# Attention, a gated feed-forward layer and a second one in one kernel: operands moved to multiples of 128 bytes, masks put ahead of the scores

## The chip, the cores and the metric

The kernel runs on one core of a Trainium2 chip. The metric is the device time of one execution in microseconds: 475.54 us, the median of three runs (475.52 to 476.49).

## The reference

Three stages follow each other. The sizes are batch 2, 12 heads, 448 positions, 64 numbers a head; 896 tokens of 768; hidden sizes 1536 and 1024.

```python
scores = (1 / sqrt(64)) * q @ k.T          # per batch and head, 448 x 448
scores = where(upper triangle, -1e9, scores)
attn = exp(scores - max(scores)); attn = attn / (sum(attn) + 1e-9)
x = (attn @ v) as 896 tokens x 768

gate = sigmoid(x @ w_gate); val = x @ w_val
x = (gate * val) @ w_out                   # 768 -> 1536 -> 768

h = x @ w_in2                              # 768 -> 1024
solu = h * softmax(h)
ln = (solu - mean(solu)) / sqrt(var(solu) + 1e-6) * g_ln
out = ln @ w_out2                          # 1024 -> 768
```

All weights come as 64-bit floats. The kernel loads them as pairs of 32-bit words and makes 32-bit floats of them by bit operations.

## The kernel before, in words

**Products.** Most matrix products are made of three terms: each operand is split into a part in the rounded 32-bit format fp32r (called hi) and the rest (lo), and hi x hi, hi x lo and lo x hi are added in PSUM. x (tiles xy), the weight chunks (hl), the gated values (g), w_in2 (wi), w_out2 (wo) and the transposed normed values (lt) are kept as such pairs.

**Attention** (lines 204 to 566) works on twelve pairs of heads, p = 0 to 11. The positions are cut into four query tiles i = 0 to 3, which need the first 64, 192, 320 and 448 keys (causal mask). For each pair:

- `sc_mask` (L320) writes the mask of some tiles into PSUM, as small bf16 products; `sc_dots` (L336) adds the scores. Tiles 3 and 0 share one PSUM tile of two banks, tiles 2 and 1 another; the pool `ps_s` has two such PSUM tiles, so a pair's masks write what the pair before has just been read from. Both heads of a pair run side by side in the two halves of TensorE's rows. From pair 3 on, tiles 1 to 3 use the three terms (tiles qks), tile 0 plain fp32 in two passes.
- `sc_max` (VectorE, L351) takes the maxima, `sc_exp` (ScalarE, L363) the exponentials into p_t with their sums, in the order of tiles 3, 0, 2, 1.
- `sums` (GpSimd), `recips` (VectorE, L371 and L372) and DMAs over DRAM (`rs_rows`, `rs_bcast`) make the reciprocals of the sums and spread them.
- `tr_mm` (TensorE, L408) transposes p_t in four units u = 0 to 3; `tr_copy` copies each unit out of PSUM, units 0 and 1 on VectorE (L419), 2 and 3 on ScalarE (L417). The units use three PSUM buffers in turn.
- `pv_mm` (TensorE, L431) multiplies with v, `x_mul` (VectorE, L437) by the reciprocals, `x_hi` (ScalarE, L441) and `x_lo` (GpSimd, L447; VectorE for the last pair) split the result into xy.
- `prep_q`, `prep_hi` and `prep_lo` (GpSimd) scale and split q and k of the pair to come.

**Order.** The table `STEPS` (L481) writes the order out by hand: an entry is a step, an engine, a function and a range of pairs, and the function runs for pair p at step 8 p + its first number. Each engine works through its own queue in that order; waits between engines are put in where data or buffers ask for them. Into this order the making of the first four weight chunks is woven: `FIRST_BITS` (steps at which one of the four bit operations of a chunk is issued: L118 on ScalarE, then L121, L123 and L126 on VectorE), `FIRST_HI` (L139, ScalarE) and `FIRST_LO` (L144, VectorE), and `EARLY` (steps at which some products of the next stage, L463, go to TensorE). The first three pairs are issued by hand ahead of the table (L499 to L528).

**Filling products.** `keep_warm` (L290) issues products of zeros: 31 at the start, 6 behind the scores of pair 0, and 8 ahead of the first transposes (L405).

**Later stages.** L601 multiplies x with w_gate and w_val, chunk by chunk; L631 the gated values with w_out; `h_mm` (L663) with w_in2; `ln_T` (L706) transposes, and `out_mm` (L724) multiplies with w_out2, in blocks of 48 products for each of seven token tiles.

**Where tiles lie.** Tiles of a pool lie one behind the other in each partition, in multiples of 32 bytes. Pools on the left begin with `const`, whose seven tiles take 512 + 512 + 256 + 512 + 256 + 32 + 32 = 2,112 bytes, 64 more than a multiple of 128. So xy, the weight rings (hl) and g, and later wo, e and the first token tile's lt, start 64 past a multiple of 128. The pools on the right (qkr, qks, `one`; later w_in2 and the other lt in `w2`) end 32 bytes below a multiple of 128, so qkr, qks and wi start 96 past one. In the pool `one`, q_sc and v_raw start at multiples of 128, p_t 32 past one.

The two lines that the change of order is about, and the ones that set an order by hand:

```python
(0, 'E', lambda p: sc_mm(p, (0, 1)), 3), (2, 'E', lambda p: sc_mm(p, (1,)), 2, 3),
(23, 'A', x_hi), (15, 'A', lambda p: tr_copy(p, 2, 'A'), 1),
(12, 'D', lambda p: tr_copy(p, 0, 'D'), 2), (21, 'D', x_mul), (14, 'D', lambda p: tr_copy(p, 1, 'D'), 1),
```

Of the kernel before, what the change touches and what calls it, by code (L numbers as in the profile page):

```python
# [10 lines left out]
F32 = mybir.dt.float32  # L11
# [8 lines left out]
B, H, S, D = 2, 12, 448, 64  # L20
# [3 lines left out]
NQ = 4  # L24
QE = [64, 192, 320, 448]
POFF = [0, 128, 512, 1152, 2048]
# [17 lines left out]
def attn_moe_moe2(ctx: ExitStack, tc: tile.TileContext, qk, v, w_gv, w_out, w_in2, w_out2, g_ln, out):  # L44
# [19 lines left out]
    mhalf = const.tile([128, 1], F32, name="mhalf")  # L64

# [138 lines left out]
    with ExitStack() as actx:  # L204
# [12 lines left out]
        SPLIT = range(3, NH // 2)  # L217
# [29 lines left out]
        q_sc = [one.tile([128, D + S], F32, name=f"qs{i}") for i in range(2)]  # L247
        v_raw = [one.tile([128, NQ, 2 * D], F32, name=f"vr{i}") for i in range(3)]
# [30 lines left out]
        p_t = [one.tile([128, POFF[NQ]], F32, name=f"p{i}") for i in range(2)]  # L279

        mx0 = {(i, e): one.tile([128, 1], F32, name=f"mx{i}{e}") for i in (0, 1, 3) for e in range(2)}

        def groups(p):
            return GROUPS if p else ((1, 0), (3,), (2,))
# [39 lines left out]
        def sc_dots(p, g):  # L324
            k = qk_raw[p][:, 1]
            for i in groups(p)[g]:
                n = QE[i]
                if p not in SPLIT or i == 0:
                    terms = [(q_sc[p % 2][:, n - D:n + D], k)]
                else:  # L330
                    t = qk_sp[p]
                    terms = [(t[:, a, n - 128:n], t[:, b]) for a, b in ((0, 2), (0, 3), (1, 2))]
                for m, (l, r) in enumerate(terms):
                    for e in range(2):
                        rows = slice(e * D, (e + 1) * D)
                        nc.tensor.matmul(out=ps_sc[p, i][1 - e], lhsT=l[rows], rhs=r[rows, S - n:] if e else r[rows, :n],  # L336
                                         start=False, stop=(m == len(terms) - 1), skip_group_check=True)

        def sc_mm(p, gs):
            for g in gs:  # L340
                sc_mask(p, g)
                sc_dots(p, g)
# [60 lines left out]
        def tr_mm(p, u):  # L403
            ps = ps_tr[p, u] = ps_t.tile([128, 512], F32, tag="t", name="t")
            if p == u == 0:  # L405
                keep_warm(ps, 8)
            for c, k in tr_blocks(u):
                nc.tensor.transpose(ps[:, max(c, 0):max(c, 0) + 128], p_t[p % 2][:, k:k + 128],  # L408
                                    ident if c >= 0 else identx)
# [42 lines left out]
        def early_tiles():  # L452

            for t in range(NE):
                g_t[t] = gpa.tile([128, 2, NT], FR, tag=f"g{t}", name=f"g{t}")
                for i in range(2):
                    ps = ps_s.tile([128, 2, 512], F32, tag="s", name="gv")[:, 0, :S]
                    for kk in range(NK):
# [15 lines left out]
        FIRST_BITS = {40: (0,), 44: (0, 0), 52: (0,), 72: (1,), 76: (1, 1), 84: (1,),  # L474
                      96: (2,), 97: (2,), 99: (2,), 101: (2,), 104: (3,), 105: (3,), 107: (3,), 109: (3,)}
        FIRST_HI, FIRST_LO = {56: 0, 88: 1}, {60: 0, 92: 1}
# [5 lines left out]
            (0, 'E', lambda p: sc_mm(p, (0, 1)), 3), (2, 'E', lambda p: sc_mm(p, (1,)), 2, 3),  # L482
# [4 lines left out]
            (16, 'A', lambda p: tr_copy(p, 3, 'A'), 1), (16, 'D', lambda p: tr_copy(p, 3, 'D'), 0, 1),  # L487
            (1, 'A', lambda p: sc_exp(p, (3,)), 2), (2, 'A', lambda p: sc_exp(p, (0,)), 2),
            (5, 'A', lambda p: sc_exp(p, (2,)), 1), (6, 'A', lambda p: sc_exp(p, (1,)), 1),
            (23, 'A', x_hi), (15, 'A', lambda p: tr_copy(p, 2, 'A'), 1), (14, 'D', lambda p: tr_copy(p, 2, 'D'), 0, 1),  # L490
            (8, 'D', recips), (9, 'D', lambda p: tr_copy(p, 0, 'D'), 1, 2), (-1, 'D', lambda p: sc_max(p, 3, 0), 2, 3), (0, 'D', lambda p: sc_max(p, 3, 0), 3),
            (2, 'D', lambda p: sc_max(p, 2), 2), (3, 'D', lambda p: sc_max(p, 1), 2),
            (12, 'D', lambda p: tr_copy(p, 0, 'D'), 2), (21, 'D', x_mul), (14, 'D', lambda p: tr_copy(p, 1, 'D'), 1),
            (7, 'P', sums, 1), (-8, 'P', prep_q, 3), (23, 'D', x_lo, NPR - 1), (-8, 'P', prep_hi, SPLIT.start, SPLIT.stop), (-7, 'P', prep_lo, SPLIT.start, SPLIT.stop),
# [6 lines left out]
        for g in range(3):  # L501
            sc_dots(0, g)
# [36 lines left out]
        for s in range(PER * NPR + 26):  # L539
# [18 lines left out]
            if s in (76, 84):  # L558
                dma_next()
# [235 lines left out]
```

## Time and profile before

| | us |
|---|---|
| median of three runs | 475.54 |
| the profiled execution | 476.21 |
| its span, first to last instruction | 474.3 |
| attention, until the products of L601 begin | 91.1 |
| TensorE busy | 468.5 |
| VectorE busy | 309.2 |
| ScalarE busy | 206.2 |
| GpSimd busy | 103.2 |

The profile is of one execution. PE is TensorE's products, PEld its weight loads, DVE VectorE, ACT ScalarE, POOL GpSimd, SP the engine that issues DMAs. The length of a product's row runs from its start to its modelled end, and products overlap in the pipe, so the spacing of starts is what they cost each other. TensorE has the granted clock 1.0 in all of the 40 slices of the page. The 1.9 us between the span and the time of the execution lie outside the first and last instruction.

### The profile page before, as it was taken

Reading aid. Unit: us, or ns where it says so; the run is one execution under the profiler, and the core shown is the slowest. Engines: PE = TensorE matmul, PEld = TensorE weight load, DVE = VectorE, ACT = ScalarE, POOL = GpSimd, SP = SyncE. Lnnn points to the kernel's source line nnn. Section 1 sums busy time; section 2 is a strip of 40 time slices with the busy share of each in tenths; the row PEclk is TensorE's granted clock in tenths of the full one; section 3 lists DMA queues with packets and bytes.
Section 4 is the critical chain, followed back from the end, with each engine's and each line's share of the span. In section 5 each row is a group of like instructions: output and inputs, shape, how many; then the busy total and the mean of one; then the engine's idle time right before and its main releaser. Section 6 shows DMA issues by size and latency. Waiting matters only on the chain.

```text
span 474.3 us, 7187 instructions
## 1 busy us (share of the span) xinstructions
PE 468.5 (99%) x2761; PEld 413.7 (87%) x2761; DVE 309.2 (65%) x476; ACT 206.2 (43%) x439; POOL 103.2 (22%) x156
## 2 busy tenths in 40 slices
PE   8999999999999999999999999999999999999997
PEld 6677766899999999999999999999988888999997
DVE  5879898457567797777875667667618888712110
ACT  5798987433335435344353243433223334332111
POOL 2588992100000000000000000000423768500000
PEclk9999999999999999999999999999999999999999
DMA  7465654322314445335453233453412230001001
GB/s 225 132 198 184 186 170 136 102 79 101 133 56 166 165 145 170 99 131 178 133 178 133 80 129 102 157 177 134 158 43 66 80 120 1 2 35 66 35 33 66
DMA packets 16546, 55.56 MB, mean 117 GB/s; under 512 B 2816, under 2 KB 5888, under 8 KB 16512
## 3 DMA queue, kind: packets, MB, share of 16 engines
q1 hardware_dynamic: 16512, 55.11, 34.9%
q8 instruction: 21, 0.34, 0.3%
q14 instruction: 13, 0.11, 0.1%
HBM read 52.30 MB, written 2.80 MB: 116 GB/s over the span
## 4 chain that ended last, share of the span: by engine, by line
PE 91%; POOL 3%; DMA 2%; DVE 1%; issue 1%; ACT 1%; SPq 0%; DVEq 0%; POOLq 0%; ACTq 0%
PE gv L601 35%; PE pm L631 18%; PE po L724 12%; PE h L663 12%; PE x L431 4%; PE t L408 3%; PE s L336 2%; DMA qkr<-in_qk_dram 2%; PE gv L463 2%; PE tp L706 1%; POOL qks L239 1%; POOL qks L234 1%; POOL qs L242 0%; POOL xy L447 0%; PE s L320 0%
## 5 line engine op out<-in xcount | busy, mean ns | idle before, releaser
L601 PE MATMUL gv<-xy,hl 128*128 128x448 f32 x828 | 168.1, 366 | 0.0
L601 PEld LDWEIGHTS gv<-xy,hl 128*128 128x128 f32 x828 | 155.6, 188 | 12.5 <-issue 0.4
L631 PE MATMUL pm<-g,hl 128*128 128x448 f32 x432 | 87.7, 366 | 0.0
L631 PEld LDWEIGHTS pm<-g,hl 128*128 128x128 f32 x432 | 81.2, 188 | 6.3
L648 POOL TENSOR_SCALAR t<-t,g_sb 128x768 f32<-128x768 f32 x8 | 9.0, 1123 | 253.6 <-PE pm L631 253.6
L144 DVE TENSOR_TENSOR hl<-t,hl 128x768 fp32r<-128x768 f32 x36 | 34.9, 969 | 39.8 <-ACT hl L139 38.1
L724 PE MATMUL po<-wo,lt 128*128 128x384 f32 x336 | 60.6, 340 | 0.0
L663 PE MATMUL h<-wi,xy 128*128 128x512 f32 x252 | 59.3, 396 | 0.0
L724 PEld LDWEIGHTS po<-wo,lt 128*128 128x128 f32 x336 | 58.7, 188 | 0.2 <-POOL wo L653 0.2
L663 PEld LDWEIGHTS h<-wi,xy 128*128 128x128 f32 x252 | 47.2, 188 | 11.3
L123 DVE SCALAR_TENSOR_TENSOR t<-raw,t 128x768 int32<-128x768 int32 (+1 forms) x56 | 54.3, 970 | 1.9
L126 DVE SCALAR_TENSOR_TENSOR t<-raw,t 128x768 int32<-128x768 int32 (+1 forms) x56 | 53.0, 946 | 1.6
L118 ACT ACTIVATE raw<-raw 128x768 f32<-128x768 f32 (+1 forms) x56 | 48.3, 870 | 11.1 <-DMA raw<-in_wo_dram 6.8
L363 ACT ACTIVATE p<-s,sum 128x320 f32<-128x320 f32 (+3 forms) x90 | 41.4, 487 | 7.3 <-DVE sum L351 5.6
L121 DVE TENSOR_SCALAR t<-raw 128x768 int32<-128x768 int32 (+1 forms) x56 | 31.7, 565 | 6.1 <-ACT raw L118 6.0
L181 DVE TENSOR_TENSOR lt<-tp,lt 128x512 fp32r<-128x512 f32 x14 | 9.7, 690 | 36.4 <-ACT lt L180 36.4
L139 ACT CAST hl<-t 128x768 fp32r<-128x768 f32 x36 | 30.0, 833 | 4.2 <-PE pm L631 4.2
L193 ACT ACTIVATE wk<-gv 128x448 f32<-128x448 f32 x23 | 11.3, 541 | 43.4 <-PE gv L601 43.4
L431 PE MATMUL x<-pt,vr 128*64 128x384 f32 (+3 forms) x168 | 28.6, 410 | 0.0
L351 DVE TENSOR_REDUCE sum<-s 128x2 f32<-128x640 f32 (+3 forms) x43 | 26.7, 678 | 0.6 <-ACT pt L417 0.3
L139 ACT CAST wi<-t 128x512 fp32r<-128x512 f32 x12 | 7.5, 621 | 42.3 <-DVE t L126 42.3
L408 PE MATMUL t<-ident,p 128*128 128x128 f32 x180 | 24.5, 277 | 0.3 <-DVE pt L419 0.3
(95 smaller groups left out, 438.1 us busy)
## 6 DMA issues: line engine op xcount, KB each, us to landing
raw<-in_gv_dram SPq DMA_DIRECT2D x22, 768.0 KB
raw<-in_wo_dram SPq DMA_DIRECT2D x20, 768.0 KB
raw<-in_wi_dram SPq DMA_DIRECT2D x12, 512.0 KB
qkr<-in_qk_dram SPq DMA_DIRECT2D x11, 448.0 KB
vr<-in_v_dram SPq DMA_DIRECT2D x12, 256.0 KB
rb<-rd SPq DMA_DIRECT2D x24, 112.0 KB
out_dram<-o SPq DMA_DIRECT2D x6, 384.0 KB
raw<-in_gv_dram SPq DMA_DIRECT2D x8, 192.0 KB
```

The costliest lines, as they stand in the source:

```text
L118: nc.scalar.activation(out=w1.bitcast(F32), in_=w1.bitcast(F32), func=AF.Copy, scale=2.0 ** -112)
L123: nc.vector.scalar_tensor_tensor(out=tt, in0=w1, scalar=-2 ** 31, in1=tt, op0=ALU.bitwise_and, op1=ALU.bitwise_or)
L126: nc.vector.scalar_tensor_tensor(out=tt, in0=w0, scalar=29, in1=tt, op0=ALU.logical_shift_right, op1=ALU.bitwise_or)
L139: nc.scalar.copy(out=hi, in_=t_t[it])
L144: eng.tensor_tensor(out=lo, in0=t_t.pop(it), in1=f32(hi), op=ALU.subtract)
L363: nc.scalar.activation(out=p_t[p % 2][:, POFF[i] + (1 - e) * n:POFF[i] + (2 - e) * n], in_=ps_sc[p, i][1 - e], func=AF.Exp, bias=mx, scale ...
L408: nc.tensor.transpose(ps[:, max(c, 0):max(c, 0) + 128], p_t[p % 2][:, k:k + 128], ident if c >= 0 else identx)
L431: nc.tensor.matmul(out=ps_pv[pr][d, q0:], lhsT=v_raw[pr % 3][:, (j - 1) % NQ, d], rhs=pt_t[pr][:, u, c0:c0 + S - q0], start=(j == 0), stop ...
L601: nc.tensor.matmul(out=ps[i, b], lhsT=w[:, a, cs], rhs=xy[kk][:, x, b * S:(b + 1) * S], start=(kk == 0 and a == 0 and x == 0), stop=(kk == ...
L631: nc.tensor.matmul(out=ps[b], lhsT=w[:, a, cs], rhs=g_t[kk][:, x, b * S:(b + 1) * S], start=(kk == 0 and a == 0 and x == 0), stop=(kk == N ...
L663: nc.tensor.matmul(out=h[:, n * 512:(n + 1) * 512], lhsT=xy[kk][:, a, tk], rhs=wi[n * NK + kk][:, c], start=(kk == 0 and i == 0), stop=(kk ...
L724: nc.tensor.matmul(out=ps[n], lhsT=lts[k // 4][:, a, k % 4], rhs=wo[k][:, c, cs], start=(k == 0 and i == 0), stop=(k == NF2 - 1 and i == 2))
```

## The change

- **Offsets.** A tile of 64 bytes that nobody uses goes behind the others of `const`, one of 96 bytes to the right end (pool `tail`), one of 32 bytes to the end of `one`; p_t moves ahead of v_raw. All operands of TensorE then start at multiples of 128 bytes.
- **Masks.** From pair 3 on, `sc_all` issues the masks of both PSUM tiles and then the scores of tiles 0, 3, 2, 1. Before it was masks of 3 and 0, scores of 3 and 0, masks of 2 and 1, scores of 2 and 1.
- **Filling products.** The eight ahead of the first transposes go.
- **Order.** `x_mul` goes from step 21 to 22, behind the copy of unit 1; `x_hi` from 23 to 24, behind the copies of units 2 and 3; the last pair's `x_lo` from 23 to 25. The bit operations of chunks 0 and 1 go to steps that are 8 apart instead of two at a time, the hi and lo parts of these chunks to later steps, one bit operation of chunk 3 from step 109 to 114, one DMA from step 84 to 93.

```diff
+    const.tile([128, 16], F32, name="fill")
+    tail = ctx.enter_context(tc.tile_pool(name="tail", bufs=1, side="right"))
+    tail.tile([128, 24], F32, name="tail")
...
         q_sc = [one.tile([128, D + S], F32, name=f"qs{i}") for i in range(2)]
+        p_t = [one.tile([128, POFF[NQ]], F32, name=f"p{i}") for i in range(2)]
         v_raw = [one.tile([128, NQ, 2 * D], F32, name=f"vr{i}") for i in range(3)]
...
-        p_t = [one.tile([128, POFF[NQ]], F32, name=f"p{i}") for i in range(2)]
 
         mx0 = {(i, e): one.tile([128, 1], F32, name=f"mx{i}{e}") for i in (0, 1, 3) for e in range(2)}
+        one.tile([128, 8], F32, name="rest")
...
-        def sc_dots(p, g):
+        def sc_dots(p, *tiles):
             k = qk_raw[p][:, 1]
-            for i in groups(p)[g]:
+            for i in tiles:
...
         def sc_mm(p, gs):
             for g in gs:
                 sc_mask(p, g)
-                sc_dots(p, g)
+                sc_dots(p, *groups(p)[g])
+
+        def sc_all(p):
+            for g in range(2):
+                sc_mask(p, g)
+            sc_dots(p, 0, 3, 2, 1)
...
         def tr_mm(p, u):
             ps = ps_tr[p, u] = ps_t.tile([128, 512], F32, tag="t", name="t")
-            if p == u == 0:
-                keep_warm(ps, 8)
...
-        FIRST_BITS = {40: (0,), 44: (0, 0), 52: (0,), 72: (1,), 76: (1, 1), 84: (1,),
-                      96: (2,), 97: (2,), 99: (2,), 101: (2,), 104: (3,), 105: (3,), 107: (3,), 109: (3,)}
-        FIRST_HI, FIRST_LO = {56: 0, 88: 1}, {60: 0, 92: 1}
+        FIRST_BITS = {40: (0,), 44: (0,), 52: (0,), 60: (0,), 72: (1,), 76: (1,), 84: (1,), 92: (1,),
+                      96: (2,), 97: (2,), 99: (2,), 101: (2,), 104: (3,), 105: (3,), 107: (3,), 114: (3,)}
+        FIRST_HI, FIRST_LO = {64: 0, 95: 1}, {68: 0, 100: 1}
...
-            (0, 'E', lambda p: sc_mm(p, (0, 1)), 3), (2, 'E', lambda p: sc_mm(p, (1,)), 2, 3),
+            (0, 'E', sc_all, 3), (2, 'E', lambda p: sc_mm(p, (1,)), 2, 3),
...
-            (16, 'A', lambda p: tr_copy(p, 3, 'A'), 1), (16, 'D', lambda p: tr_copy(p, 3, 'D'), 0, 1),
+            (16, 'A', lambda p: tr_copy(p, 3, 'A'), 1), (24, 'A', x_hi), (16, 'D', lambda p: tr_copy(p, 3, 'D'), 0, 1),
...
-            (23, 'A', x_hi), (15, 'A', lambda p: tr_copy(p, 2, 'A'), 1), (14, 'D', lambda p: tr_copy(p, 2, 'D'), 0, 1),
+            (15, 'A', lambda p: tr_copy(p, 2, 'A'), 1), (14, 'D', lambda p: tr_copy(p, 2, 'D'), 0, 1),
...
-            (12, 'D', lambda p: tr_copy(p, 0, 'D'), 2), (21, 'D', x_mul), (14, 'D', lambda p: tr_copy(p, 1, 'D'), 1),
-            (7, 'P', sums, 1), (-8, 'P', prep_q, 3), (23, 'D', x_lo, NPR - 1), (-8, 'P', prep_hi, SPLIT.start, SPLIT.stop), (-7, 'P', prep_lo, SPLIT.start, SPLIT.stop),
+            (12, 'D', lambda p: tr_copy(p, 0, 'D'), 2), (14, 'D', lambda p: tr_copy(p, 1, 'D'), 1), (22, 'D', x_mul),
+            (7, 'P', sums, 1), (-8, 'P', prep_q, 3), (25, 'D', x_lo, NPR - 1), (-8, 'P', prep_hi, SPLIT.start, SPLIT.stop), (-7, 'P', prep_lo, SPLIT.start, SPLIT.stop),
...
-            if s in (76, 84):
+            if s in (76, 93):
                 dma_next()
```

## Rows read from the trace of the kernel before

**Rows 1.** The page's busy line: engine, busy us, share of the span, instructions

```profile
PE 468.5 (99%) x2761; PEld 413.7 (87%) x2761; DVE 309.2 (65%) x476; ACT 206.2 (43%) x439; POOL 103.2 (22%) x156
```

**Rows 2.** Groups by line: form, count, busy us, mean ns, idle before and releaser

```profile
L601 PE MATMUL gv<-xy,hl 128*128 128x448 f32 x828 | 168.1, 366 | 0.0
L663 PE MATMUL h<-wi,xy 128*128 128x512 f32 x252 | 59.3, 396 | 0.0
L724 PE MATMUL po<-wo,lt 128*128 128x384 f32 x336 | 60.6, 340 | 0.0
L724 PEld LDWEIGHTS po<-wo,lt 128*128 128x128 f32 x336 | 58.7, 188 | 0.2 <-POOL wo L653 0.2
...
L336 PE MATMUL s<-qks 64*128 64x448 f32 x54 | 7.7, 388 | 0.0
```

**Rows 3.** Timeline of TensorE in the last stage: start us, us, instructions

```profile
407.30 8.74 PE L724 MATMUL po<-wo,lt 128*128 128x384 f32 x48
...
416.66 8.69 PE L724 MATMUL po<-wo,lt 128*128 128x384 f32 x48
```

**Rows 4.** Timeline of TensorE, pair 5 and the start of pair 6

```profile
32.38 0.26 PE L320 MATMUL s<-mk_r,mk_l 64*128 64x64 bf16 x6
32.48 0.85 PE L336 MATMUL s<-qks 64*128 64x448 f32 x6
33.16 0.33 PE L336 MATMUL s<-qkr,qs 64*128 64x64 f32 x4
33.33 0.28 PE L320 MATMUL s<-mk_r,mk_l 64*128 64x64 bf16 x8
...
38.62 0.26 PE L320 MATMUL s<-mk_r,mk_l 64*128 64x64 bf16 x6
```

**Rows 5.** Timeline of ScalarE, end of pair 4's exponentials, pair 5's first and last

```profile
32.71 0.24 ACT L363 ACTIVATION_READ_ACCUMULATOR p<-s,sum 128x1 f32 x1
...
35.06 0.68 ACT L363 ACTIVATE p<-s,sum 128x448 f32<-128x448 f32 x1
...
38.57 0.28 ACT L363 ACTIVATION_READ_ACCUMULATOR p<-s,sum 128x1 f32 x1
```

**Rows 6.** Timelines of ScalarE and TensorE in pair 3

```profile
20.56 0.21 ACT L363 ACTIVATION_READ_ACCUMULATOR p<-s,sum 128x1 f32 x1
...
20.83 0.29 PE L320 MATMUL s<-mk_r,mk_l 64*128 64x64 bf16 x8
```

**Rows 7.** Timeline of VectorE in pair 5

```profile
33.32 0.20 DVE L371 RECIPROCAL rs32t<-rs8i 128x8 f32<-128x8 f32 x1 [1.02 <-POOL rs8i L367]
...
33.69 2.44 DVE L351 TENSOR_REDUCE sum<-s 128x2 f32<-128x896 f32 x4
...
36.58 1.26 DVE L121 TENSOR_SCALAR t<-raw 128x768 int32<-128x768 int32 x1
37.88 1.79 DVE L123 SCALAR_TENSOR_TENSOR t<-raw,t 128x768 int32<-128x768 int32 x1
```

**Rows 8.** Timeline of ScalarE, end of pair 10's exponentials

```profile
71.48 0.24 ACT L363 ACTIVATION_READ_ACCUMULATOR p<-s,sum 128x1 f32 x1
```

**Rows 9.** Timelines of TensorE and VectorE in the first pairs

```profile
10.51 0.62 PE L290 MATMUL t<-idle 128*128 128x128 bf16 x8
10.97 0.28 PE L408 MATMUL t<-identx,p 128*128 128x128 f32 x1
...
17.44 1.29 DVE L351 TENSOR_REDUCE sum<-s 128x2 f32<-128x640 f32 x2 [0.26 <-PE s L336]
```

**Rows 10.** Timelines of ScalarE, VectorE and TensorE at the end of attention

```profile
73.35 0.84 ACT L139 CAST hl<-t 128x768 fp32r<-128x768 f32 x1
...
79.14 0.96 ACT L118 ACTIVATE raw<-raw 128x768 f32<-128x768 f32 x1
...
81.61 0.62 DVE L419 COPY pt<-t 128x448 f32<-128x448 f32 x1
...
82.28 0.66 PE L408 MATMUL t<-ident,p 128*128 128x128 f32 x4 [0.28 <-DVE pt L419]
```

More of the change, by code (lines that the diff above doesn't have):

```diff
@@ L501, in attn_moe_moe2 @@
         for g in range(3):
-            sc_dots(0, g)
+            sc_dots(0, *groups(0)[g])
         load_qk(3)
```

## The prediction

> **What bounds the kernel now.** I read the page's busy line first, then the costliest groups, then the timelines of the engines. TensorE is busy 468.5 of 474.3 us [rows 1], at a granted clock of 1.0 (the 2.4 GHz level) in all 40 slices. So time can come from only two places: products that run faster, or moments in which TensorE stands still behind a wait. I take both in turn, since the change touches both: the padding of the tiles touches the first, everything in the attention part the second.
>
> *Speed of the products.* 828 products of 448 columns take 168.1 us, 203 ns each; 252 of 512 columns 59.3 us, 235 ns; 336 of 384 columns 60.6 us, 180 ns [rows 2]. One column per cycle at 2.4 GHz would be 187, 213 and 160 ns: 16 to 22 ns lie on top of each. Before the change x, the weight halves hl, g and wo stand 64 bytes past a multiple of 128, w_in2 and (but for the first token tile) lt 96 past, the split q and k 96 past. The only place where one kind of product is seen with two offsets is the last stage: the first token tile reads lt at 64, the others at 96. A block of 48 products takes 8.74 for the first, which holds a 0.2 wait for wo [rows 2], so 8.54; the second takes 8.69 [rows 3]. That is 0.15 us in 48, 3 ns each, for 32 bytes.
>
> *Waits in attention.* In pair 5 TensorE does masks of tiles 3 and 0 (32.38), tile 3 (32.48), tile 0 (33.16), masks of 2 and 1 (33.33), tiles 2 and 1, and comes round again at 38.62: 6.24 us a pair [rows 4]. ScalarE's exponentials of pair 4's last tile end at 32.95 (32.71 + 0.24) [rows 5]. They free the PSUM tile that the masks of 2 and 1 write, so these masks at 33.33 have 0.4 to spare. In pair 3 there was nothing to spare: the exponentials end at 20.77 and the masks start at 20.83, 0.05 later [rows 6]. I call this end E.
>
> **The change part by part.**
>
> *Padding.* lt from 96 to 0 in six of seven token tiles: 6 x 0.15 = 0.9 us at most; 0.54 if the first tile's wait was shorter than it reads; I take 0.7. w_in2 from 96: at the rate of the 448-column products (203 x 512 / 448 = 232 ns) the 512-column ones lose 3 ns, x 252 = 0.8; I take 0.6. For the 1,260 products of the two large stages (and wo) all offsets go from 64 to 0, and no row shows an operand of this kind at 0. Bounds: nothing, or the whole 16 ns x 1,260 = 20 us, with the 20 and 22 ns of the others some 30 us; a loss as dear as the 3 ns seen is the other end (+3.8). I take 0, since both operands already have the same offset here and 64 is the better one in rows 3. Sum -1.3.
>
> The Trainium skill bears on this twice. Its page "TensorE: Matmul & The Clock Gate", section "Back-to-back issue gap", gives N/2.4 + 2.5 ns, which is 189 ns for 448 columns; rows 2 have 203, so here the rule misses by 14 ns, and if the offset were the reason, this is what comes back (the rival named last). Its page "SBUF — State Buffer", section "Specifications (TRN2)", speaks of 16-byte cachelines, by which 64 and 96 are as good as 0 and the padding gives nothing; rows 3 speak against it, by 0.15 us a block.
>
> *Masks ahead, tile 0 first.* The masks of tiles 2 and 1 now come 0.1 after those of 3 and 0, not 0.95. They still wait for E. In pair 5 they would be ready at 32.48 and E is 32.95: TensorE would stand 0.5, and tiles 0, 3, 2 and 1 are queued behind. The waits spared in exchange are small: a weight load is uncovered behind short masks (tile 3's three pairs take 0.68 where 3 x 0.203 = 0.61 would do), and this happens once a pair instead of twice; but tile 0, now first, has its own load uncovered and is too short to cover tile 3's, 0.17 + 0.08 + 0.06 = 0.31 (bounds 0.17 and 0.33).
> Does TensorE's lateness go round? The loop after the change: E, 0.05 to the masks [rows 6], 0.12 for them [rows 4], 0.31 for tile 0, 0.61 for tile 3, 0.18 until its results stand (a row of 0.388 against a spacing of 0.203 [rows 2]) = 1.27, then the maximum, which needs tiles 3 and 0 together. From there 1.37 to the first exponential (33.69 [rows 7] to 35.06 [rows 5]) and 3.79 to the next E (38.57 + 0.28 [rows 5]): 6.43 in all. Now the maximum starts 0.75 after E (32.95 to 33.69), held by the reciprocals and not by TensorE, and the loop of 5.9 is shorter than TensorE's 6.24. So TensorE sets the pace before, this loop after: 8 x 6.43 = 51.4 from the E of pair 2 (20.77) to that of pair 10 (71.72 [rows 8]), against 50.95, +0.5.
>
> *Bit steps spread out.* Two steps in one pair (1.26 and 1.79 [rows 7]) now fill VectorE past the next reciprocals; such pairs are why 50.95 is more than 8 x 6.24 = 49.9. Spread one to a pair, a step of 1.0 fits into the 1.02 that VectorE is free ahead of the reciprocals [rows 7]; the slow form (1.79) still delays the maximum, from nothing to 0.4: I take 0.15 in three pairs, +0.45.
>
> *No filling products.* The eight take 10.51 to 10.97 on TensorE [rows 9], 0.46; the transposes behind them read exponentials that are done. ScalarE and VectorE cover part: VectorE idles only 0.26 for TensorE before pair 2's maxima [rows 9]. E of pair 2 comes 0.26 to 0.46 earlier, I take -0.35. Without this cover nothing else fills it; the gap is far too short to matter elsewhere.
>
> *Copies ahead of x; moved weight steps.* The copy of unit 1 already waits for its transposes, so swapping it with the multiply gives nothing; ScalarE's copies come 0.46 earlier, and nobody waits for them in a full pair. x_mul, now behind a copy, still comes before the next product into its single PSUM buffer. At the end it costs: hi of chunk 1 (0.84 [rows 10]) moves from a gap in pair 11 to between the last unit copies, ahead of the L118 at 79.14. From that one hangs a chain: VectorE's two steps, the copy at 81.61, and TensorE at 82.28, which already waits 0.28 [rows 10]. All of 0.84 falls on it (bounds 0 and 0.84, nearer the upper since nothing there is idle): +0.8.
>
> Attention: +0.5 + 0.45 - 0.35 + 0.8 = +1.4 (bounds -0.5 and +2.5). With the padding -1.3: +0.1. The profiled execution took 476.21 (span 474.3 and 1.9 around it), so 476.3; the median of the runs is 0.67 lower, 475.54, so **475.6**.
>
> **The rivals.**
> *The wait is dearer and padding gives nothing.* E decides in every pair from 3 to 11, and 64, 96 and 0 are alike: 475.5 + 1.4 to 2.1 = 476.9 to 477.6. For it: three pairs already wait for E (pair 3 in rows 6). Against: rows 3. It decides from the point where the loop passes 6.24.
> *The wait doesn't bite.* If the maximum starts before tile 3 is complete, or the exponentials gain on TensorE once the bit steps are spread, the loop stays near 5.9, TensorE keeps its 6.24, and 8 x 6.24 = 49.9 with a chain at the end that is hidden: attention -0.2, padding -1.3, 474.0. Against: before the change the maximum already waits for both tiles by program order.
> *Padding also pays from 64.* 3 ns x 1,260 = 3.8 more: 471.8. For it, the 16 ns that nothing explains; against, products at 64 and 96 have nearly the same surplus.
> *The whole surplus goes.* 30 us less, 1.4 more: 447. Against it the same near equality.
>
> **How the numbers follow.** Forecast 0.40 (its own range 474.7 to 476.5), first rival 0.25, second 0.17, third 0.11, last 0.07. What can be told from no change here is 0.2%, 0.95 us. Faster: the last three and a little of the forecast, 0.36; slower: the first rival and a little of the forecast, 0.28; the rest 0.36. The range 471.5 to 477.6 leaves out the last rival and the ends of the first and third.
>
> **What would show it.** Right: in pairs 4 to 10 the masks of tiles 2 and 1 start 0.05 after E; a pair lasts about 6.4; the last-stage blocks of 48 are all near 8.55 and the 512-column products near 232 ns; the 448-column ones stay at 203; TensorE waits over 0.8 for a VectorE copy near 83. Wrong: 448-column products clearly under 203 (the padding rivals), pairs of 6.2 (the wait doesn't bite), or lt blocks unchanged at 8.69.

## The result, and the profile after

The changed kernel takes 482.17 us, the median of four runs (477.0 to 482.61), against 475.84 before (four runs, 475.52 to 476.49). The ratio on record, over all the runs and not of the two medians, is 1.0105, 95% interval 1.0082 to 1.0128. The forecast was 475.6, with 471.5 to 477.6 as its range. One of the four runs, at 477.0, stands 5 us away from the other three (481.75 to 482.61); what that is turned out to be the main thing here.

The page after, busy line and chain by line (lines move by 4 to 9: L601 is now L608, L631 L638, L663 L670, L724 L731, L320 L324, L363 L372):

```profile
PE 474.1 (99%) x2753; PEld 414.3 (86%) x2753; DVE 306.8 (64%) x476; ACT 205.9 (43%) x439; POOL 103.8 (22%) x156
...
PE gv L608 36%; PE pm L638 19%; PE po L731 12%; PE h L670 12%; ACT p L372 7%; PE s L340 3%; DVE sum L360 2%; PE tp L713 1%; PE gv L470 1%; PE x L438 1%; PE t L415 1%; PE warm L294 1%; PE s L324 1%; ACT pt L424 0%; DVE t L126 0%
```

TensorE is still busy nearly all the time, but ScalarE's exponentials now hold 7% of the chain that ended last. The groups by line, in answer to [rows 2]:

```profile
L608 PE MATMUL gv<-xy,hl 128*128 128x448 f32 x828 | 171.4, 368 | 0.0
...
L638 PE MATMUL pm<-g,hl 128*128 128x448 f32 x432 | 89.4, 368 | 0.0
...
L731 PE MATMUL po<-wo,lt 128*128 128x384 f32 x336 | 60.2, 337 | 0.0
L670 PE MATMUL h<-wi,xy 128*128 128x512 f32 x252 | 59.1, 395 | 0.0
```

The 828 products were 168.1 us and are 171.4. The 432 of L638 (L631 before) were 87.7. So 3.3 + 1.7 = 5.0 us went into products that were valued at no change. The 384- and 512-column products gain 0.4 and 0.2. The rest is attention. Timeline of TensorE: the end of attention with its wait, then one unbroken stretch of the large stage, then two blocks of the last stage in answer to [rows 3]:

```profile
84.47 0.66 PE L415 MATMUL t<-ident,p 128*128 128x128 f32 x4 [0.70 <-DVE pt L426]
...
93.33 8.94 PE L608 MATMUL gv<-xy,hl 128*128 128x448 f32 x42
...
149.64 110.73 PE L608 MATMUL gv<-xy,hl 128*128 128x448 f32 x535
...
414.28 8.77 PE L731 MATMUL po<-wo,lt 128*128 128x384 f32 x48
423.69 8.61 PE L731 MATMUL po<-wo,lt 128*128 128x384 f32 x48
```

The large stage starts at 93.33 instead of 91.14, 2.2 us late. With the 5.0 and less 0.7 that is the 6.5 by which the span grew (474.3 to 480.8). The long stretch gives the spacing from start to start: (110.73 - 0.37) / 534 = 206.7 ns, one product like the other. The same reading in the trace before:

```profile
149.82 50.42 PE L601 MATMUL gv<-xy,hl 128*128 128x448 f32 x248
```

That is (50.42 - 0.37) / 247 = 202.6 ns; over the whole stage it is 202.7, and five products follow each other at about 199, 207, 203, 202 and 203 ns. Both patterns last through both large stages. The difference, 4.0 ns x 1,260, is 5.0 us, and the single run at 477.0 is 5 us faster than its sisters. I call the patterns the slow and the fast rhythm of the kernel. Only a profiled execution shows its rhythm; for the others it is read from the 5 us.

The loop that the prediction worked out for attention is in the chain of waits of the changed kernel (start us, us, what):

```profile
39.73 0.55 ACT p L372 x2
40.28 0.04 issue
40.33 0.29 PE s L324 x8
40.62 0.95 PE s L340 x10
41.57 0.02 issue
41.59 1.30 DVE sum L360 x2
42.90 0.02 issue
42.92 0.04 ACTq L372
42.95 0.05 issue
43.00 3.17 ACT p L372 x13
46.17 0.04 issue
46.21 0.55 ACT p L372 x2
```

The exponentials end (40.28), the masks start 0.05 later, the maximum at 41.59, the first exponential at 43.00, the end at 46.76: 6.48 a pair, with TensorE waiting inside it.

### The profile page after: what moved, and what is told of

It is laid out like the page before. It is cut to its first block, busy times and chain, and to the rows that moved or that the text cites. A ratio compares the mean times of both kernels' runs of the same rounds, so it can differ in the third digit from the quotient of the medians.

```text
span 480.8 us, 7190 instructions
## 1 busy us (share of the span) xinstructions
PE 474.1 (99%) x2753; PEld 414.3 (86%) x2753; DVE 306.8 (64%) x476; ACT 205.9 (43%) x439; POOL 103.8 (22%) x156
## 4 chain that ended last, share of the span: by engine, by line
PE 88%; ACT 8%; DVE 3%; issue 0%; ACTq 0%; DVEq 0%
PE gv L608 36%; PE pm L638 19%; PE po L731 12%; PE h L670 12%; ACT p L372 7%; PE s L340 3%; DVE sum L360 2%; PE tp L713 1%; PE gv L470 1%; PE x L438 1%; PE t L415 1%; PE warm L294 1%; PE s L324 1%; ACT pt L424 0%; DVE t L126 0%
## 5 line engine op out<-in xcount | busy, mean ns | idle before, releaser
L608 PE MATMUL gv<-xy,hl 128*128 128x448 f32 x828 | 171.4, 368 | 0.0
L608 PEld LDWEIGHTS gv<-xy,hl 128*128 128x128 f32 x828 | 155.4, 188 | 16.0 <-issue 0.4
L638 PE MATMUL pm<-g,hl 128*128 128x448 f32 x432 | 89.4, 368 | 0.0
L638 PEld LDWEIGHTS pm<-g,hl 128*128 128x128 f32 x432 | 81.1, 188 | 8.2
L731 PE MATMUL po<-wo,lt 128*128 128x384 f32 x336 | 60.2, 337 | 0.0
L670 PE MATMUL h<-wi,xy 128*128 128x512 f32 x252 | 59.1, 395 | 0.0
L731 PEld LDWEIGHTS po<-wo,lt 128*128 128x128 f32 x336 | 58.2, 188 | 0.2 <-POOL wo L660 0.2
L670 PEld LDWEIGHTS h<-wi,xy 128*128 128x128 f32 x252 | 47.3, 188 | 10.9
L126 DVE SCALAR_TENSOR_TENSOR t<-raw,t 128x768 int32<-128x768 int32 (+1 forms) x56 | 52.8, 942 | 1.9
L129 DVE SCALAR_TENSOR_TENSOR t<-raw,t 128x768 int32<-128x768 int32 (+1 forms) x56 | 51.3, 915 | 1.6
L372 ACT ACTIVATE p<-s,sum 128x320 f32<-128x320 f32 (+3 forms) x90 | 41.4, 483 | 12.0 <-PE t L415 7.6
```

Source lines behind the costliest of these rows:

```text
L126: nc.vector.scalar_tensor_tensor(out=tt, in0=w1, scalar=-2 ** 31, in1=tt, op0=ALU.bitwise_and, op1=ALU.bitwise_or)
L129: nc.vector.scalar_tensor_tensor(out=tt, in0=w0, scalar=29, in1=tt, op0=ALU.logical_shift_right, op1=ALU.bitwise_or)
L372: nc.scalar.activation(out=p_t[p % 2][:, POFF[i] + (1 - e) * n:POFF[i] + (2 - e) * n], in_=ps_sc[p, i][1 - e], func=AF.Exp, bias=mx, scale ...
L608: nc.tensor.matmul(out=ps[i, b], lhsT=w[:, a, cs], rhs=xy[kk][:, x, b * S:(b + 1) * S], start=(kk == 0 and a == 0 and x == 0), stop=(kk == ...
L638: nc.tensor.matmul(out=ps[b], lhsT=w[:, a, cs], rhs=g_t[kk][:, x, b * S:(b + 1) * S], start=(kk == 0 and a == 0 and x == 0), stop=(kk == N ...
L670: nc.tensor.matmul(out=h[:, n * 512:(n + 1) * 512], lhsT=xy[kk][:, a, tk], rhs=wi[n * NK + kk][:, c], start=(kk == 0 and i == 0), stop=(kk ...
```

## Experiments

**Offsets alone and order alone, a disturbed stream, the old mask order.** The first four kernels part the change into its pieces. The code is shortened: `...` and a comment stand for what is left out.

`e1_pad_only`: the kernel before with the padding only.

```diff
+    const.tile([128, 16], F32, name="fill")
...
+    tail.tile([128, 24], F32, name="tail")          # pool at the right end
...
+        p_t = ...                                   # ahead of v_raw
...
+        one.tile([128, 8], F32, name="rest")
```

> Only the offsets of the change, the order of the kernel before. Theory A (a 448-column product costs 4 ns more when both operands lie at multiples of 128 bytes): 206.7 ns a product in both large stages, 1,260 x 4.0 = +5.0 us; the 512- and 384-column products 1.0 and 1.8 ns faster, -0.25 and -0.5; attention as before: about 480.1, in every execution. Theory B (448-column products have two steady rhythms, 202.7 and 206.7 ns, and what happens when the first one of the stage enters decides which is kept): each execution is either about 475.1 or about 480.1, and none lies between. Theory C (the order of the change makes the slow rhythm, not the offsets): 202.7 in every execution, about 475.1.

Twelve executions: five at 475.1 to 475.6, seven at 479.6 to 480.8, none between. The profiled one (480.09) is in the slow rhythm (171.4 and 89.4 us again). That is theory B, and the order of the change is not needed for it. In the fast rhythm the padding gains about 0.7 us.

`e2_order_only`: the changed kernel without fill, tail and rest, p_t at its old place.

> Only the order of the change (masks ahead, no filling products, moved steps), the offsets of before. The trace after has the first product of the large stage 2.2 us later. Theory A (offsets make the 206.7): 202.7 ns, 475.8 + 2.2 = 478.0. Theory B (two rhythms, the entry decides): 478.0 or 483.0 run by run; if the 64-byte offset, whose products vary more from one to the next, also shakes a product out of the slow rhythm, always 478.0. Theory C (order alone): 206.7 in every execution, 483.

478.17 (478.06 to 478.47, five executions), ratio 1.0049 (1.0037 to 1.0061), 202.7 ns a product in the trace; all five near the time of the fast rhythm.

`e3_after_step`: the changed kernel with two short products of 64 columns (`step_off`), whose result a product of the stage overwrites. (The condition put them ahead of hidden tile 1, the second of the twelve 128-wide blocks of the hidden size, 36 products into the stage, not ahead of its first product as the expectations say; so too in e5, e7 and e8.)

```diff
+                if t == NE and i == 0:
+                    step_off(ps[0, 1], w[:, 0, :128], xy[0][:, 0, :D])
```

> The changed kernel with two 64-column products ahead of the first 448-column product of the large stage, which they write and which starts its sum anew. They cost 0.1 us. Theory A: nothing else, 448-column products stay at 206.7, 482.3. Theory B: the rhythm is entered from another point; if it is then the 202.7 one, 1,260 x 4.0 = 5.0 us come back: 477.2 in all executions, or more of them than in the changed kernel.

477.04 to 477.85 in five executions, with the same offsets as the changed kernel: 4.4 us below its median. In its trace the stage was fast from the first product on, ahead of the short ones; here only the count speaks, five of five against one of four.

`e4_after_old_masks`: masks and scores in the old order.

```diff
-            (0, 'E', sc_all, 3), ...
+            (0, 'E', lambda p: sc_mm(p, (0, 1)), 3), ...
```

> The changed kernel, but from pair 3 on with masks of 3 and 0, scores of 3 and 0, masks of 2 and 1, scores of 2 and 1 as before. If the loop over the freed PSUM tile (6.47 us a pair in the trace after, 6.37 before) is what attention lost between pair 2 and pair 11, 1.3 to 1.6 us come back there and the first product of the large stage starts near 91.8 instead of 93.3; the 1.0 us lost behind pair 11's exponentials stays. Rival: the masks are not what holds the pairs, and it starts near 93.3. Total by the rhythm of the 448-column products: 480.7 or 475.7 with the gain.

Two executions at 473.8 and 474.7, ten at 478.6 to 480.4. The large stage starts at 89.84, 3.5 us earlier than in the changed kernel and 1.3 earlier than before. TensorE, two pairs:

```profile
38.07 0.26 PE L324 MATMUL s<-mk_r,mk_l 64*128 64x64 bf16 x6
...
39.01 0.28 PE L324 MATMUL s<-mk_r,mk_l 64*128 64x64 bf16 x8
...
44.31 0.26 PE L324 MATMUL s<-mk_r,mk_l 64*128 64x64 bf16 x6
```

A pair is 6.24 again, without a wait: in pairs 7 to 11 TensorE sets the pace (pairs 3 to 6 take 5.86 to 6.31), since bit steps no longer come two at a time; in the kernel before, the two pairs that had two took 7.34 and 7.39. From pair 2's end to pair 10's it is 49.1 us, 50.95 before, 52.2 in the changed kernel. So the masks ahead cost 3.1 there, more than was expected of this run, and the spread steps, with the other moved ones, gain 1.8.

**Does the disturbance do it, and what does each edit of attention cost?**

`e5_old_masks_step`: the two kernels above, e3 and e4, in one.

> The changed kernel with the old order of masks and scores and the two 64-column products ahead of the first 448-column product of the large stage. Theory B (two rhythms, the entry decides): 202.7 ns a product in every execution, first product of the stage near 89.9, about 474.0, none near 479. If the two short products helped by chance in five executions: some executions near 479.

473.94 to 474.71 in seven executions, none near 479; ratio 0.9967 (0.9956 to 0.9978). The trace shows the switch (TensorE; L188 are the short products):

```profile
90.02 7.70 PE L610 MATMUL gv<-xy,hl 128*128 128x448 f32 x36
97.56 0.30 PE L188 MATMUL gv<-xy,hl 128*128 128x64 f32 x2
97.70 102.59 PE L610 MATMUL gv<-xy,hl 128*128 128x448 f32 x505
```

Behind the first interval the 36 are 206.7 ns apart; behind the short ones it is (102.59 - 0.37) / 504 = 202.8. e7 and e8 show the same.

`e6_step_midway`: the changed kernel, the short products at hidden tile 6 (`t == 6`).

> The changed kernel with the two 64-column products not at the start of the large stage but half way, ahead of the first product of hidden tile 6. Theory B: where the stage has entered the slow rhythm, 396 products at 206.7 ns, then 432 and the 432 of the next stage at 202.7: 864 x 4.0 = 3.4 us less than the changed kernel, about 478.8; where it entered the fast one, 477.1 or, if the two products can also lead into the slow one, 480.6. Rival (something at the start, such as the transfers under way, holds the products at 206.7): no change at tile 6, 482.2.

The profiled execution (479.43) entered the slow rhythm and shows the switch later in the stage:

```profile
93.39 82.10 PE L610 MATMUL gv<-xy,hl 128*128 128x448 f32 x396
175.33 0.30 PE L188 MATMUL gv<-xy,hl 128*128 128x64 f32 x2
175.47 87.79 PE L610 MATMUL gv<-xy,hl 128*128 128x448 f32 x432
```

Ahead of the two, 82.10 us for 396, 206.7 ns apart (the first interval, 0.31, and the last product's 0.37 left out); behind them 87.79 for 432, 202.8. The tiles and their offsets are the same. The other three executions, at 478.0, fit one that was fast from the start.

`e7_small_first`: only the 64-key tile ahead of the 448-key tile, base e5.

```diff
+            sc_mask(p, 0)
+            sc_dots(p, 0, 3)
+            sc_mask(p, 1)
+            sc_dots(p, 2, 1)
```

> As the kernel with the old order of masks and the two short products, but the scores of the 64-key tile go ahead of those of the 448-key tile; the masks of 2 and 1 stay behind both. Theory: putting all masks ahead of all scores is what makes the loop over the freed PSUM tile decide; the order of two tiles behind one mask group only uncovers weight loads, some 0.1 us a pair: periods of 6.24 to 6.35, 474.0 to 475.0. Rival: the 64-key tile first costs most of the 3.5 us that the two orders differ by: periods near 6.47, 477.

475.1 (474.64 to 475.18), pairs of 6.3: 0.7 above e5. So of the 3.5 us of the new order some 0.6 is the tile order, the rest the masks put ahead.

`e8_chunk1_as_before`: base e5, chunk 1's steps as before.

```diff
-        FIRST_BITS = {... 72: (1,), 76: (1,), 84: (1,), 92: (1,),
+        FIRST_BITS = {... 72: (1,), 76: (1, 1), 84: (1,),
...
-        FIRST_HI, FIRST_LO = {64: 0, 95: 1}, {68: 0, 100: 1}
+        FIRST_HI, FIRST_LO = {64: 0, 88: 1}, {68: 0, 92: 1}
```

> As the kernel with the old order of masks and the two short products, but the bit steps, the hi and the lo part of chunk 1 at the steps of before (two bit steps in one pair, hi in pair 11). In the traces of the changed kernel and of the old mask order the first product of the large stage comes 14.25 us behind pair 11's last exponential, in the kernel before 13.25. Theory (the hi part of chunk 1 between the last unit copies is what costs it): 13.3 again, -1.0, and one pair of some 0.5 more for the doubled bit steps: 473.5. Rival (the moved multiply and x_hi steps cost it): 14.25 stays and the doubled step is added: 474.5.

474.8 (474.6 to 475.49, eleven), 0.4 above e5. Both terms are there: pair 11's exponentials end 1.0 later (the doubled step holds one pair, 7.32 against 6.24), the way from there to the large stage is 0.7 shorter. The hi step's price was about right; the doubled step is dearer than was expected.

**What makes an execution slow?**

`e9_x64_w0`: base e4; the 64 unused bytes lie behind xy instead of ahead of it. `e10_x0_w64`: 64 ahead of it and 64 behind.

```diff
+    xyp.tile([128, 16], F32, name="fill2")          # behind the xy tiles; e9 without fill, e10 with it
```

> The changed kernel with the old mask order (no short products), but the 64 unused bytes lie behind xy instead of ahead of it: xy, the moving operand of the first large stage, is 64 bytes past a multiple of 128, the weights and g are at multiples. With both at multiples 10 of 12 executions were near 479, 2 near 474.2. If it takes both operands at multiples of 128 to be held at 206.7 ns, or the moving one: none or few near 479 for the first stage (the second stage, both at multiples, could still enter on its own: 475.5 to 476). If the weights (stationary) alone decide: 206.7 ns and near 479 in most executions. If offsets have no part in it: 479 in most.

> The reverse: xy at multiples of 128, the weight halves and g 64 bytes past one (64 unused bytes ahead of xy and 64 behind it). If both must be at multiples, or the stationary operand: 202.7 ns in all executions, near 474.2. If the moving operand alone decides: 206.7 ns in the first stage in most executions, 202.7 again when the second begins (there the moving g is at 64): near 477.5. If offsets have no part in it: near 479 in most.

475.82 (475.19 to 476.07, eleven) and 475.5 (474.55 to 476.07, twelve), none near 479. In both traces L608 (L609) is 167.7 us for 828, 202.2 ns, a third pattern (about 199, 201, 207), which no expectation had; the second stage, whose two operands have equal offsets, is slow, 89.4. That is why e10 lies 1.3 above the 474.2 expected.

`e11_step_at_start`: base e4, the short products ahead of the very first (`if c == 0`).

> All offsets at multiples of 128, old mask order, and the two 64-column products now ahead of the very first 448-column product of the large stage instead of 36 products into it. If any two short products ahead lead into the fast rhythm: 202.7 ns from the first product on, 474.2 in every execution, 0.1 less than with the later place. If the two only help because they come in the middle of a running stream: some executions near 479.

Nine executions at 473.9 to 474.7, three at 478.9 to 479.4. At the start they help less than in the stream, where none of 34 executions (e3, e5, e7, e8) was slow.

`e12_left_at_64`: base e4 without fill, so xy, weights and g are at 64 as before the change.

> The changed kernel with the old mask order and without the 64 unused bytes of the constants: the pools on the left (xy, weights, g, later wo) at 64 as before the change, those on the right (split q and k, w_in2, lt) at multiples of 128. Theory: 448-column products at 202.7 in every execution as in the kernel before, without any short product; the 512-column products keep their gain of 1.0 ns and the 384-column ones theirs of 1.8 (0.7 us in all) if it comes from the right side: 474.2. If that gain needs the left side at multiples too: 474.9.

Seven at 474.4 to 475.4, five at 479.6 to 480.4. My theory fell here: both operands at 64, and by their times five are slow all the same (the profiled execution was a fast one). Multiples of 128 are not what the slow rhythm needs.

`e13_before_kicks`: the kernel before, untouched but for short products in the stream.

```diff
+                for n in {2: (64,), 4: (64, 64), 6: (64, 64, 64), 8: (128,), 10: (256,)}.get(t, ()) if i == 0 else ():
+                    nc.tensor.matmul(out=ps[0, 0][:, :n], lhsT=w[:, 0, :128], rhs=xy[0][:, 0, :n], start=True, stop=True)
```

> The kernel before, all its offsets, with extra short products in the running stream of the large stage: one of 64 columns ahead of hidden tile 2, two ahead of tile 4, three ahead of tile 6, one of 128 columns ahead of tile 8, one of 256 ahead of tile 10. Theory B without offsets (two rhythms belong to any stream of these products whose two operands have the same offset; the phase at entry decides): in the trace some of the stretches behind a disturbance run at 206.7 ns though all offsets are those of before; two short products should lead to 202.7, as in the changed kernel. Theory A' (at 64 and 64, with the right side at 96, the slow rhythm doesn't exist): all stretches at 202.7, 477 at most (1.2 of added products and loads).

477.62 (476.98 to 478.17). Timeline of TensorE:

```profile
113.61 0.19 PE L595 MATMUL gv<-xy,hl 128*128 128x64 f32 x1
113.64 29.42 PE L603 MATMUL gv<-xy,hl 128*128 128x448 f32 x144
142.89 0.30 PE L595 MATMUL gv<-xy,hl 128*128 128x64 f32 x2
143.03 29.42 PE L603 MATMUL gv<-xy,hl 128*128 128x448 f32 x144
172.29 0.42 PE L595 MATMUL gv<-xy,hl 128*128 128x64 f32 x3
172.54 30.00 PE L603 MATMUL gv<-xy,hl 128*128 128x448 f32 x144
202.38 0.22 PE L595 MATMUL gv<-xy,hl 128*128 128x128 f32 x1
202.44 29.40 PE L603 MATMUL gv<-xy,hl 128*128 128x448 f32 x144
231.67 0.28 PE L595 MATMUL gv<-xy,hl 128*128 128x256 f32 x1
231.79 29.35 PE L603 MATMUL gv<-xy,hl 128*128 128x448 f32 x144
```

Five stretches of 144 products. Behind three short ones it is 30.00, 0.58 longer, 4.0 ns each, until a product of 128 columns brings the fast rhythm back. The kernel before has the slow rhythm too, with every offset of before; it only never enters it by itself (none of 118 executions, 475.3 to 476.8). The other six executions of e13 took 477.0 to 477.8; which of them entered it can't be read from their times.

`e14_pt_only`, `e15_pad_not_pt`, `e18_right_only`: the kernel before with p_t moved alone; with all of the padding but p_t; with the right side's padding alone.

> The kernel before, with nothing changed but p_t moved ahead of v_raw, so that it starts at multiples of 128 and not 32 past one. If p_t's offset, through the transposes ahead of the large stage, is what makes the slow rhythm reachable: some of the executions near 480.8 (about half in the kernel with all of the padding), the others near 475.9. If the right-hand pools' ends or the left side are: all within 475.3 to 476.8.

> The kernel before with all of the padding, but p_t left where it was, 32 bytes past a multiple of 128. If p_t is what makes the slow rhythm reachable: 202.7 ns in all executions, about 475.3, none near 480. If the other tiles are (xy, weights, split q and k at multiples): some near 480, as with all of the padding (7 of 12).

> The kernel before with the padding of the right side alone (split q and k, w_in2 and most of lt at multiples of 128); the left pools at 64 and p_t at 32 as before. If the right side is enough to make the slow rhythm reachable: some or all executions near 480.5, though every operand of the 448-column products lies as before. If it takes the left side or p_t too: all executions at 475.4, of which 0.5 less than before comes from lt.

475.97 (eleven, none slow), 480.39 (five, all slow: 480.1 to 480.8), 475.8 (eleven, none slow). Neither p_t nor the right side alone leads to the slow rhythm; the left side alone was not run.

The offsets below are bytes past a multiple of 128: left is xy, the weights, g and wo, right is qkr, qks, w_in2 and most of lt. An execution is counted as slow by its time.

| kernel | left, right, p_t past 128 | order | slow of all |
|---|---|---|---|
| before | 64, 96, 32 | before | 0 of 118 |
| e14 | 64, 96, 0 | before | 0 of 11 |
| e18 | 64, 0, 32 | before | 0 of 11 |
| e2 | 64, 96, 32 | changed | 0 of 5 |
| e12 | 64, 0, 0 | changed, old masks | 5 of 12 |
| e4 | 0, 0, 0 | changed, old masks | 10 of 12 |
| e1 | 0, 0, 0 | before | 7 of 12 |
| after | 0, 0, 0 | changed | 3 of 4 |
| e15 | 0, 0, 32 | before | 5 of 5 |

The rows come from several chips (e1, e2 and e4 from one, e14, e15 and e18 from a second, e12 from a third; the kernel before ran beside each of them), so shares of different rows, such as e1 and e15, are compared across chips. And none of five, as in e2, would come up once in 15 times even with the share of e12.

**A kernel that beats both.** `e16_weights_64`: base e10, and 64 unused bytes ahead of g, so that in both large stages the stationary operand is 64 past a multiple and the moving one at a multiple. `e17_hi_late`: on top of it chunk 1's hi at step 97, its lo at 102.

> The changed kernel with the old mask order and without short products; the weight halves (stationary in both large stages) 64 bytes past a multiple of 128, xy and g (moving) at multiples. With one pair 64 bytes apart the first stage ran at 202.2 ns in the trace and never entered the slow rhythm, in 23 executions; the second stage, whose two operands had the same offset, was at 206.7. If the distance of 64 bytes between the two operands is what prevents it: 202.2 in both stages, in every execution; 474.4 - 1,260 x 0.45 = about 473.8. If the second stage enters a slow rhythm whatever its offsets, from the other rhythm of the first: 475.5.

> The kernel with the weight halves at 64 (moving operands at multiples, old mask order), with one step moved: the hi part of chunk 1 goes behind ScalarE's first step of chunk 2 instead of ahead of it, its lo part (VectorE) behind the last unit copies. If the hi part ahead of that step is what delays the chain at the end of attention, as the prediction had it: the step starts 0.84 us earlier, the copy behind it too, TensorE's wait of 0.52 for that copy goes, and the first product of the large stage comes 0.5 earlier: 472.2. Rival: the lo part, now behind the copies and needed by the early products, takes its place, or TensorE waits for the exponentials instead: 472.7 or more.

e16: 472.67 (471.95 to 473.6, five), ratio 0.9928 (0.9915 to 0.994). Groups of e10, then of e16:

```profile
L609 PE MATMUL gv<-xy,hl 128*128 128x448 f32 x828 | 167.7, 364 | 0.0
L639 PE MATMUL pm<-g,hl 128*128 128x448 f32 x432 | 89.4, 368 | 0.0
```

```profile
L610 PE MATMUL gv<-xy,hl 128*128 128x448 f32 x828 | 167.7, 364 | 0.0
L640 PE MATMUL pm<-g,hl 128*128 128x448 f32 x432 | 86.6, 362 | 0.0
```

One edit, 64 bytes ahead of g, takes the second stage from 206.7 to 200.0 ns a product, 2.8 us, and the time falls by as much. That is better than expected: a fourth pattern (about 197, 202, 201). e17: 472.02 (471.67 to 472.78, five), ratio 0.9917 (0.9904 to 0.9931). The wait for VectorE's copy is gone; the timeline of TensorE in e16 and in e17:

```profile
80.42 0.66 PE L417 MATMUL t<-ident,p 128*128 128x128 f32 x4 [0.52 <-DVE pt L428]
...
89.28 1.08 PE L610 MATMUL gv<-xy,hl 128*128 128x448 f32 x4
```

```profile
79.23 1.55 PE L417 MATMUL t<-ident,p 128*128 128x128 f32 x12
...
88.97 0.88 PE L610 MATMUL gv<-xy,hl 128*128 128x448 f32 x3
```

The stage starts 0.3 earlier in these two executions, but in that of e17 the whole of attention runs late: pair 11's exponentials end at 75.46, in e16 at 75.04. From their end to the stage it is 13.51 against 14.24, 0.7 less, which is what the medians show (0.65).

## Why the prediction was wrong

The step that failed is the padding of the 448-column products, "I take 0". It measured +5.0 us, beyond the bound of +3.8 that the text itself gave as its other end. The step took offsets for a fixed price per product, and that is wrong in kind: the same tiles at the same offsets run at 202.7 or 206.7 ns (e5, e6, e13), and an execution keeps what it entered. The padding moved the kernel from one that was never seen to enter the slow rhythm (0 of 118, and 0 of 5 with the new order) to one that often does (3 of 4, and 7 of 12 with the old order). None of the rivals was this; "padding also pays" had the sign the other way. How far the median lies off is in part the draw: the one execution at 477.0 lies inside the range.

- *lt and w_in2, -1.3.* -0.7: blocks of 48 fell from 8.69 to 8.61 (-0.5 in six), and the 512-column products by 1.0 ns (-0.25). The sum for w_in2 began too high: 235 ns is busy time over count, while the products of the trace before follow each other at 233.4 (232.4 after). Nor is the gain w_in2's alone: with w_in2 at a multiple and xy at 64 (e9, e12, e18) the 252 products take 59.3 as before, with both at multiples 59.0 to 59.2. For lt, the load's wait lengthens two intervals of the first block to 285 and 186 ns where 174 is usual, 0.12 us and not 0.2, so rows 3 hold 0.07 a block, half of what was read. Nor is there a fixed price for lt's 32 bytes, as the reading of [rows 3] had it. In e18 lt lies at a multiple and wo at 64, and the 336 products take what they took before; in e16 the same two offsets give 0.5 less. The groups of e18, then of e16:

```profile
L727 PE MATMUL po<-wo,lt 128*128 128x384 f32 x336 | 60.6, 339 | 0.0
L666 PE MATMUL h<-wi,xy 128*128 128x512 f32 x252 | 59.3, 396 | 0.0
```

```profile
L733 PE MATMUL po<-wo,lt 128*128 128x384 f32 x336 | 60.1, 338 | 0.0
```

- *The loop, 6.43 a pair.* 6.47. The mechanism stood as written: masks 0.05 behind the exponentials' end, 1.31 to the maximum (1.27 predicted), 1.41 to the first exponential (1.37), then 3.76 (3.79). From pair 2's end to pair 10's it took 52.2 against 50.95 before: +1.3, where +0.5 and +0.45 were given; pair 4 alone was 6.93, which I did not trace to its cause (it was longer than its neighbours before the change too, 6.31 against 5.86 and 5.91). From pair 10 to pair 11 it took another 0.3 more.
- *Bit steps spread, +0.45.* Wrong in kind. No pair but the fourth strays from 6.47, and with the old mask order (e4) the spread steps, with the other moved ones, gain 1.8 us from pair 2 to pair 10, where the masks ahead then cost 3.1. So +0.5 and +0.45 come near the measured +1.3 by luck: the first was too small, the second had the wrong sign.
- *No filling, -0.35.* Pair 2's exponentials end 0.38 earlier (20.40 against 20.78). Between executions this end varies by more: 20.2 to 21.4 in the six traces with the eight products, 19.5 to 20.4 in the fourteen without, with means 0.5 apart. The mean granted clock is 0.999 to 1.0 in these traces, with them and without.
- *hi of chunk 1, +0.8.* TensorE's wait is 0.70 where it was 0.28, and from pair 11's last exponential to the large stage it is 1.0 longer (14.25 against 13.26). e8 and e17 each give back 0.7 of it, so the mechanism and the price were right. The rest is VectorE's first bit step behind it, which takes 0.80 instead of 0.56.

Attention together: +2.2 against +1.4, inside its bounds of -0.5 and +2.5. Without the slow rhythm the changed kernel is at 477.0 to 477.9 (its execution at 477.0 and e3), at the upper end of the range and about where the first rival was (476.9 to 477.6), whose first half is what happened: the exponentials' end decides in every pair.

What stays open: by which way the padded tiles set the phase in which TensorE arrives at the large stage. In all of the traces but that with the short products at the start (e11) the last product of attention starts 309 or 310 ns ahead of the first of the stage, without a wait, and at equal offsets the first interval of the stage was 309 or 310 ns where the fast rhythm followed, 307, 308, 313 or 314 where the slow one did. A few nanoseconds tell the two apart; that they decide is not shown, and what shifts them was not found. Why a distance of 64 bytes between the operands goes with spacings of 202.2 and 200.0 ns is open too.

## What to carry to other kernels

Before a change is charged with a few nanoseconds per product, look at the list of its times: two clusters with a fixed distance can be one kernel in two rhythms, and a median of few runs tells only which was drawn. Where a stream is bound by products, vary the distance between the operands' offsets, here 64 bytes between stationary and moving, and measure many executions; alignment to round numbers is no aim in itself. And a wait put ahead of a queue of work becomes a loop with everything behind it: add the loop up, as was done for the 6.43, before moving it there.

## What the runs showed of the hardware

- Streams of weight load and product of one kind have several steady spacings at a granted clock of 1.0: for 448 columns 200.0, 202.2, 202.7 and 206.7 ns, for 384 columns 173.6 to 176.5, for 512 columns 232.1 to 233.5 (means of one token tile). In the slow rhythm each load starts 204 or 205 ns ahead of its product; in the fast one the lead runs through 195 to 205.
- The Trainium skill's page "TensorE: Matmul & The Clock Gate", section "Back-to-back issue gap", says that in a stream of loads and products both set the spacing. These traces agree in so far as the rhythms differ in how the two follow each other (the leads above). The formula that the prediction took from it is given there for the isolated gap, 189 ns for 448 columns; it is not reached in any of these streams, the nearest being 200.0.
- In the running stream two products of 64 columns always led to the fast rhythm (six traces, in four of them out of the slow one). In the one trace of e13, three led from the fast to the slow one, one of 128 back to the fast; one of 64 and one of 256 left the fast one as it was.
